# Block sums of the tokens: made over one long chunk or inside the first unit that needs them

## The chip, the cores and the metric

The program runs on one NeuronCore of a Trainium2 chip. TensorE (PE) multiplies, VectorE (DVE) and ScalarE (ACT) do element work between SBUF and the PSUM banks, SyncE (SP) issues plain DMA transfers in the order of its queue, and GpSimd (POOL) issues the accumulating ones and some plain ones. The metric is device time in microseconds for one launch, the median of several runs. A profiled execution of the same program gives the trace that is read below; its times count from the start of the span.

## The reference, cut to what matters

A linear attention over 4 x 576 tokens in 8 heads gives x, 2304 tokens by 512. Two wide layers follow, and these fill most of the time:

```python
x = attention(q, k, v, w_phi)                    # (2304, 512)
gate = 1.0 / (1.0 + np.exp(-(x @ w_gate)))       # w_gate: 512 x 1536
y = (gate * (x @ w_val)) @ w_out                 # layer 1
h = y @ w_in                                     # w_in: 512 x 2048
out = np.maximum(0.01 * h, h) @ w_out2           # layer 2
```

All of it is in fp32 (the weights arrive as 64-bit words and are taken apart on the chip).

## The kernel before, in words

Every fp32 product is made of three PE passes over a high and a low part (L52, L53, L54: high by high, low by high, high by low). ACT makes a high part with a cast, DVE the low part with a subtraction (L48 and L49 for what a unit hands on, called gh and gl).

The tokens stand in five blocks: 0 to 3 with 512 tokens each, and block B (index 4) with 256. The hidden width of a layer is worked through in chunks of 256: six for layer 1 (0 to 5), eight for layer 2 (0 to 7). Chunk 0 of layer 1 runs beside the attention, block by block. Chunk 1 is *plain*: `up_plain` for each of the five blocks, and one step of the weight stream and of the side work behind every group. From chunk 2 on, two blocks make a pair (pair 0 is blocks 0 and 1, pair 1 is blocks 2 and 3), and `quad` computes the two products of a pair in a Strassen-like form: seven products of halves for eight, with sums of the weights (`sh`, `sl`) and sums of the tokens T1 to T4. A *unit* is a pair or block B within a chunk; a pair's unit in layer 1 is two quads, first the gate's, then the value's. The units of chunk 2 are pair 1, B, pair 0, and so back and forth.

The sums of a pair are four DVE subtractions of 128x1024 (`sum_steps`, L739), and for each of the four sums one ACT cast (L749) and one DVE subtraction (L750) into two slots of 128x1024. `ts` holds the sums of one pair. The other pair's lie in HBM (`td`): L756 stores them from the SP queue, and `load_sums` (L791) reads them back from the POOL queue into the same slots, each as soon as its last use is over (`swap`). There are 41 slots of 128x1024 in all, handed out by `take` and returned by `give`; weights, sums and staging share them.

Layer 1's results are gathered in HBM: ACT copies a piece from its PSUM bank into a staging half (L678), and POOL adds it to `accd` (L679). In the last chunk the gathered values are loaded (`acc<-accd`, L663), DVE adds the last piece from PSUM (L682), and ACT and DVE split the result into the xh and xl that layer 2 reads (L685, L686).

Order is set by the text of the program, which each engine follows in its own queue. Down products (`down1_piece`) wait in `pend` and are put between the up products by `gap`; `rooms` says how many at each of a quad's six places. `ahead(n)` takes n steps of `side` (a generator, such as the making of sums) and of the weight stream (`decoded`), and the stream goes on only while more than `reserve` slots are free beside those it takes. A raw weight (`raw`, 512 KB) is loaded by SP at L122, taken apart by DVE at L102 to L114, and its sums are made at L176 to L181. Up products land in the `ps_u` banks (five), down products in the `ps_p` banks (three).

In a quad the order of names is s1 (a copy of a bank by ACT), u2, u3, then the four results; the additions are DVE's (L831), and the value's quad multiplies into the tanh of the gate's (L878).

Of the kernel before, what the change touches and what calls it, by code (L numbers as in the profile page):

```python
# [9 lines left out]
F32 = mybir.dt.float32  # L10
# [9 lines left out]
def linear_attention_moe(ctx, tc, q, k, v, w_phi, w_gate, w_val, w_out, w_in2, w_out2, out):  # L20
# [56 lines left out]
    def give(*slots):  # L77
        free.extend(place for _, place in slots)
# [501 lines left out]
    pools["q"] = ctx.enter_context(tc.tile_pool(name="q", bufs=6))  # L580
# [13 lines left out]
    fixed, halves = [], []  # L594

    def fix(n):
        for _ in range(n):
            s = take(F32)
            fixed.append(s)
            halves.extend(s[0][:, 512 * i:512 * i + 512] for i in range(2))  # L600

    fix(3)
    staged = [0]

    def staging():
        staged[0] += 1
        return halves[staged[0] % 6]
# [123 lines left out]
    td = {}  # L731
# [26 lines left out]
    def first_sums(pair, stay):  # L758

        for i in range(2):  # L760
            for j in range(2):
                s = sums[0, 2 * pair + i, j] = take(F32, "acc")
                nc.sync.dma_start(out=s[0].rearrange("p (k t) -> p k t", k=2), in_=xd[2 * pair + i][:, 2 * j:2 * j + 2])
        for _ in range(14):
            yield True
        yield from sum_steps(1, pair)
        held = deque()

        def put():
            n, s = held.popleft()  # L770
            store_sums(1, pair, n, s)
            if not stay:
                give(*s)

        for n in (2, 1, 3, 4):
            s = [take(F32R) for _ in range(2)]
            sum_parts(1, pair, n, s)
            if stay:
                ts[n] = s
            held.append((n, s))  # L780
            yield True
            yield True
            if len(held) == 2:
                put()
        for _ in range(4):
            yield True
        put()
# [9 lines left out]
    def swap(l, pair, n):  # L797

        ts[n] = [retake(s) for s in ts[n]]
        if (l, pair, n) in td:  # L800
            load_sums(l, pair, n)
        else:
            sum_parts(l, pair, n, ts[n])
            store_sums(l, pair, n, ts[n])
# [66 lines left out]
    def up_pair1(c, pair, between, then):  # L871
        h, th = {}, {}
        for i, t in quad(1, c, 0, pair, (1, 1, 1, 1, 1, 0), lambda n: None):
            th[i] = halves[6 + i]
            nc.scalar.activation(out=th[i], in_=t, func=ACTF.Tanh, scale=0.5)
        between()
        for i, t in quad(1, c, 1, pair, (1, 1, 1, 0, 0, 0), then):
            nc.vector.scalar_tensor_tensor(out=th[i], in0=th[i], scalar=1.0, in1=t, op0=ALU.add, op1=ALU.mult)  # L878
            hidden(h, (i // 2, 2 * pair + i % 2), th[i])
        return h  # L880
# [45 lines left out]
    side.append(first_sums(0, False))  # L926
    for b in range(NB):
        reserve[0] = (4, 8, 8, 5, 2)[b]
        if b == 2:
            for g in side:  # L930
                for _ in g:
                    pass
            side[:] = [first_sums(1, True)]
        h = up_plain(1, 1, b, 5)
        gap(100)
        if b in (1, 3):
            drop_x((b, 0))
        pend.extend(down1_piece(1, b, e, h) for e in range(KD))
    for g in side:
        for _ in g:  # L940
            pass
    side.clear()
    fix(2)
# [3 lines left out]
    pend.append(lambda: drop(1, 1, 2))  # L947

    units = [1, B, 0]
    keep = lambda n: None  # L950
    for c in range(2, NC1):
# [3 lines left out]
        for n, u in enumerate(units):  # L955
            if u == B:
                h = up_plain(1, c, B, 2)
            elif not final:
                h = up_pair1(c, u, (lambda: drop(1, c, 0)) if n == 2 else (lambda: None),
                             (lambda k, u=u: swap(1, 1 - u, k)) if n == 0 else keep)  # L960
            elif u == 0:
                hold[0] = 2, 0
                h = up_pair1(c, 0, lambda: None, lambda k: swap(1, 1, k))
            else:
                def between():
                    gap(100)
                    drop_sums(1, c, 0)
                    give(*fixed[:3])
                    side.append(sum_steps(2, 0))

                def then(k):
                    for g in side:
                        for _ in g:
                            pass
                    side.clear()
                    swap(2, 0, k)
                load_acc(0)
                load_acc(1)
                hold[0] = 2, 1
                h = up_pair1(c, 1, between, then)  # L980
                drop_sums(1, c, 1)
                for b in (2, 3, B):
                    load_acc(b)
                reserve[0] = 0
# [10 lines left out]
    give(*fixed[3:])  # L995

    need(2, 0, 0)
    for _ in sum_steps(2, 1):
        pass
    units = [0, B, 1]  # L1000
    for c in range(NC2):
        for n, u in enumerate(units):
            if u == B:
                h = up_plain(2, c, B, 1)
                gap(3)
            else:
                h = up_pair2(c, u, (lambda k, u=u: swap(2, 1 - u, k)) if n == 0 else keep)
                gap(100)
# [40 lines left out]
```

## Time and profile before

| | us |
|---|---|
| median of 3 runs | 1058.68 (1053.5 to 1058.72) |
| profiled execution | 1057.37 |
| its span | 1055.6 |
| outside the span | 1.77 |
| PE busy in the span | 1024.2 (97%) |
| DVE busy | 779.7 (74%) |
| ACT busy | 519.4 (49%) |
| POOL busy | 170.2 (16%) |

The time is close to PE's busy time, so what can be won without taking work from PE is what PE loses in waits and at a lower clock. Chunk 1 runs from 309.8 us to about 392 us, chunks 2 to 5 follow to about 680 us, and layer 2 fills the rest.

### The profile page before, as it was taken

The page shows a single profiled execution, that of the slowest core. Times are in us where ns is not written, and L with a number is a line of the kernel's source. Part 1 is how long each engine was busy: PE and PEld are TensorE (multiplying, and loading weights), DVE is VectorE, ACT ScalarE, POOL GpSimd, SP SyncE. Part 2 cuts the span into 40 slices and gives each one's busy share as a digit, 9 for nine tenths or more (in the row PEclk, how much of TensorE's full clock was granted, in tenths as well). Part 3 has the DMA queues.
Part 4 walks back from the last instruction along what each step waited for, and adds up shares of the span by engine and source line. Part 5 has one row for each costly group of instructions (what it writes and reads, how often), then busy time and mean ns, then how long its engine had stood idle before and what let it go on. Part 6 is the DMA issues. An engine that isn't in the chain of part 4 may idle for free.

```text
span 1055.6 us, 15004 instructions
## 1 busy us (share of the span) xinstructions
PE 1024.2 (97%) x5410; PEld 870.9 (82%) x5410; DVE 779.7 (74%) x1373; ACT 519.4 (49%) x1066; POOL 170.2 (16%) x217
## 2 busy tenths in 40 slices
PE   8999999999999989999999999899999999999998
PEld 7788989889788778888888878688888888888886
DVE  4964878766489748396684959998797887979555
ACT  4766676767456535454454434477343333433221
POOL 0112121212201123324144120001010010101000
PEclk9999999999999999999999999999999999999999
DMA  6543344332287978759499494536161542515143
GB/s 146 157 98 90 88 101 108 82 104 75 74 296 226 343 141 246 114 145 262 73 239 195 82 317 182 182 139 228 52 237 71 171 149 91 178 62 179 42 165 133
DMA packets 119481, 160.06 MB, mean 152 GB/s; under 512 B 68720, under 2 KB 71408, under 8 KB 119408
## 3 DMA queue, kind: packets, MB, share of 16 engines
q1 hardware_dynamic: 95216, 94.09, 28.5%
q0 software_dynamic: 24192, 65.02, 24.6%
q8 instruction: 43, 0.70, 0.3%
q14 instruction: 30, 0.25, 0.1%
HBM read 109.64 MB, written 49.36 MB: 151 GB/s over the span
## 4 chain that ended last, share of the span: by engine, by line
PE 81%; DVE 8%; DMA 5%; ACT 3%; issue 2%; SPq 1%; POOL 1%; POOLq 0%; DVEq 0%; ACTq 0%
PE ps_u L53 11%; PE ps_u L52 11%; PE ps_u L54 11%; PE ps_p L52 11%; PE ps_p L54 11%; PE ps_p L53 11%; PE kv L395 4%; PE ps_n L445 2%; DMA raw<-in_moe_w_gate_dram 1%; DMA acc<-xd 1%; PE ps_t L328 1%; DVE w L750 1%; DVE ql L430 1%; DVE acc L739 1%; DMA w<-td 1%
## 5 line engine op out<-in xcount | busy, mean ns | idle before, releaser
L831 DVE TENSOR_TENSOR q<-ps_u,q 128x512 f32<-128x512 f32 x160 | 109.6, 686 | 65.6 <-PE ps_u L54 59.4
L53 PE MATMUL ps_u<-xl,w 128*128 128x512 f32 (+1 forms) x432 | 151.6, 351 | 0.3 <-DVE xl L686 0.3
L52 PE MATMUL ps_u<-xh,w 128*128 128x512 f32 (+1 forms) x432 | 151.4, 351 | 0.1
L54 PE MATMUL ps_u<-xh,w 128*128 128x512 f32 (+1 forms) x432 | 150.9, 350 | 0.0
L901 DVE TENSOR_TENSOR acc<-acc,ps_p 128x512 f32<-128x512 f32 x126 | 86.1, 684 | 39.6 <-PE ps_p L54 39.0
L52 PE MATMUL ps_p<-w,gh 128*128 128x512 f32 x288 | 112.2, 390 | 0.0
L53 PE MATMUL ps_p<-w,gh 128*128 128x512 f32 x288 | 112.0, 389 | 0.0
L54 PE MATMUL ps_p<-w,gl 128*128 128x512 f32 x288 | 111.7, 389 | 0.0
L791 POOL DMA_DIRECT2D w<-td x88 | 48.7, 560 | 380.6 <-PE ps_u L54 365.2
L679 POOL DMA_DIRECT2D accd<-w x80 | 70.8, 892 | 229.2 <-ACT w L678 148.3
L52 PE MATMUL ps_u<-w 128*128 128x512 f32 x256 | 100.2, 391 | 1.6 <-DVE q L831 1.6
L53 PE MATMUL ps_u<-w 128*128 128x512 f32 x256 | 99.9, 390 | 0.7 <-DMA w<-td 0.7
L54 PE MATMUL ps_u<-w 128*128 128x512 f32 x256 | 99.7, 389 | 0.0
L52 PEld LDWEIGHTS ps_u<-xh,w 128*128 128x128 f32 x432 | 81.9, 190 | 11.9 <-DVE q L831 0.5
L53 PEld LDWEIGHTS ps_u<-xl,w 128*128 128x128 f32 x432 | 82.0, 190 | 11.4 <-DVE xl L686 0.5
L54 PEld LDWEIGHTS ps_u<-xh,w 128*128 128x128 f32 x432 | 81.9, 190 | 10.9
L52 PE MATMUL ps_p<-gh,w 128*128 128x512 f32 (+1 forms) x216 | 79.3, 373 | 10.3 <-ACT gh L48 4.8
L467 POOL TENSOR_TENSOR rb<-u,rb 64x576 f32<-64x576 f32 x32 | 49.2, 1537 | 233.8 <-DMA rb<-rd 136.3
L717 ACT ACTIVATE q<-q 128x512 f32<-128x512 f32 x48 | 30.2, 632 | 111.9 <-DVE q L831 111.6
L53 PE MATMUL ps_p<-gl,w 128*128 128x512 f32 (+1 forms) x216 | 80.1, 372 | 0.4 <-DVE gl L49 0.4
L54 PE MATMUL ps_p<-gh,w 128*128 128x512 f32 (+1 forms) x216 | 79.7, 370 | 0.0
L49 DVE TENSOR_TENSOR gl<-q,gh 128x512 fp32r<-128x512 f32 (+1 forms) x102 | 61.8, 613 | 20.6 <-ACT gh L48 20.2
(151 smaller groups left out, 2306.0 us busy)
## 6 DMA issues: line engine op xcount, KB each, us to landing
w<-td POOLq DMA_DIRECT2D x88, 512.0 KB, 6.5
td<-w SPq DMA_DIRECT2D x32, 512.0 KB, 5.2
accd<-w POOLq DMA_DIRECT2D x64, 256.0 KB, 6.1
raw<-in_moe_w_out_dram SPq DMA_DIRECT2D x28, 512.0 KB, 4.8
raw<-in_moe_w_in_dram SPq DMA_DIRECT2D x16, 512.0 KB, 4.1
raw<-in_moe_w_gate_dram SPq DMA_DIRECT2D x12, 512.0 KB, 5.9
raw<-in_moe_w_val_dram SPq DMA_DIRECT2D x12, 512.0 KB, 5.1
rb<-rd SPq DMA_DIRECT2D x32, 144.0 KB, 3.2
```

The costliest lines, as they stand in the source:

```text
L49: nc.vector.tensor_tensor(out=lo, in0=src, in1=hi.bitcast(F32), op=ALU.subtract)
L52: nc.tensor.matmul(ps, lh, rh, start=first, stop=False, **kw)
L53: nc.tensor.matmul(ps, lh, rl, start=False, stop=False, **kw)
L54: nc.tensor.matmul(ps, ll, rh, start=False, stop=last, **kw)
L395: nc.tensor.matmul(ps[:, h], p.kf[j // 2][:, j % 2, h, s, :], vf[:, j, 64 * h:64 * h + 65], start=(h, j) == (0, 0), stop=False)
L445: nc.tensor.matmul(ps2, w[0], x[0], start=s == 0, stop=s == 1)
L467: nc.gpsimd.tensor_tensor(out=p.rb[sl], in0=p.u[h][sl], in1=p.rb[sl], op=ALU.mult)
L679: nc.gpsimd.dma_start(out=accd[b][:, e], in_=st, accum_op=ALU.add)
L717: nc.scalar.activation(out=th, in_=t, func=ACTF.Lrelu)
L791: nc.gpsimd.dma_start(out=ts[n][k][0].bitcast(F32), in_=td[l, pair, n][:, k])
L831: nc.vector.tensor_tensor(out=o, in0=x, in1=y, op=ALU.add)
L901: nc.vector.tensor_tensor(out=a, in0=a, in1=po, op=ALU.add)
```

## The change

It moves the making of the token sums, and the room that this needs.

- In chunk 1 only one pair's sums are made, pair 1's, from start to end of the chunk, and they stay in `ts`. Before, pair 0's were made in blocks 0 and 1, stored and given up, and pair 1's from block 2 on.
- Pair 0's tokens are loaded when chunk 1's weights have been dropped (`load_x(0)`), and its sums are made by `make_sums(1, 0, used)` as a side step within the first unit of chunk 2, in the slots of pair 1's, each after its last use. They need no reload there: the eight `w<-td` loads of that swap are gone (88 before, 80 after).
- At the border of the layers, pair 0's sums of layer 2 are side steps of the last value quad, and pair 1's are side steps of layer 2's first unit; before, pair 0's came in one piece at each last use, and the four L739 of pair 1 ahead of layer 2's first quad.
- tanh is written in place (for three of four results) and no longer into fixed staging halves; the `q` ring has seven buffers for six, and there are two fixed slots for three and later five, with four staging halves for six.
- One down piece goes to an earlier place in a quad (rooms), and `reserve` in chunk 1 is lower, so weights may be taken apart further ahead.

```diff
--- before.py
+++ after.py
@@ -577,7 +577,7 @@
     free.extend((wpb, f"v{i}") for i in range(NSLOT - 24))
     pools["dec"] = ctx.enter_context(tc.tile_pool(name="dec", bufs=1))
     pools["hp"] = ctx.enter_context(tc.tile_pool(name="hp", bufs=6))
-    pools["q"] = ctx.enter_context(tc.tile_pool(name="q", bufs=6))
+    pools["q"] = ctx.enter_context(tc.tile_pool(name="q", bufs=7))
     ps_b = ctx.enter_context(tc.tile_pool(name="ps_b", bufs=1, space=PS))
     banks = {"u": [(ps_m, "pg"), (ps_m, "pv")] + [(ps_b, f"u{i}") for i in range(3)], "p": [(ps_m, "po"), (ps_b, "p1"), (ps_b, "p2")]}
     turn = {"u": 0, "p": 0}
@@ -591,20 +591,13 @@
         return pools["q"].tile([128, 512], F32, tag="q", name="q")[:, :w]
 
 
-    fixed, halves = [], []
-
-    def fix(n):
-        for _ in range(n):
-            s = take(F32)
-            fixed.append(s)
-            halves.extend(s[0][:, 512 * i:512 * i + 512] for i in range(2))
-
-    fix(3)
+    fixed = [take(F32) for _ in range(2)]
+    halves = [s[0][:, 512 * i:512 * i + 512] for s in fixed for i in range(2)]
     staged = [0]
 
     def staging():
         staged[0] += 1
-        return halves[staged[0] % 6]
+        return halves[staged[0] % 4]
 
     xs = {}
     for key in xh:
@@ -755,36 +748,42 @@
         for k in range(2):
             nc.sync.dma_start(out=td[l, pair, n][:, k], in_=s[k][0].bitcast(F32))
 
-    def first_sums(pair, stay):
+    def load_x(pair):
 
         for i in range(2):
             for j in range(2):
-                s = sums[0, 2 * pair + i, j] = take(F32, "acc")
-                nc.sync.dma_start(out=s[0].rearrange("p (k t) -> p k t", k=2), in_=xd[2 * pair + i][:, 2 * j:2 * j + 2])
+                t = sums[0, 2 * pair + i, j] = take(F32, "acc")
+                nc.sync.dma_start(out=t[0].rearrange("p (k t) -> p k t", k=2), in_=xd[2 * pair + i][:, 2 * j:2 * j + 2])
+
+    def make_sums(l, pair, used):
+
+        yield from sum_steps(l, pair)
+        late = None
+        for n in (2, 1, 3, 4):
+            while used is not None and n not in used:
+                yield True
+            ts[n] = [take(F32R) for _ in range(2)] if used is None else [retake(t) for t in ts[n]]
+            sum_parts(l, pair, n, ts[n])
+            yield True
+            yield True
+            if late:
+                store_sums(*late)
+            late = l, pair, n, ts[n]
+        for _ in range(2):
+            yield True
+        store_sums(*late)
+
+    def first_sums(pair):
+        load_x(pair)
         for _ in range(14):
             yield True
-        yield from sum_steps(1, pair)
-        held = deque()
-
-        def put():
-            n, s = held.popleft()
-            store_sums(1, pair, n, s)
-            if not stay:
-                give(*s)
-
-        for n in (2, 1, 3, 4):
-            s = [take(F32R) for _ in range(2)]
-            sum_parts(1, pair, n, s)
-            if stay:
-                ts[n] = s
-            held.append((n, s))
-            yield True
-            yield True
-            if len(held) == 2:
-                put()
-        for _ in range(4):
-            yield True
-        put()
+        yield from make_sums(1, pair, None)
+
+    def finish():
+        for g in side:
+            for _ in g:
+                pass
+        side.clear()
 
     def load_sums(l, pair, n):
         for k in range(2):
@@ -797,11 +796,7 @@
     def swap(l, pair, n):
 
         ts[n] = [retake(s) for s in ts[n]]
-        if (l, pair, n) in td:
-            load_sums(l, pair, n)
-        else:
-            sum_parts(l, pair, n, ts[n])
-            store_sums(l, pair, n, ts[n])
+        load_sums(l, pair, n)
 
     def quad(l, c, i, pair, rooms, then):
 
@@ -870,11 +865,11 @@
 
     def up_pair1(c, pair, between, then):
         h, th = {}, {}
-        for i, t in quad(1, c, 0, pair, (1, 1, 1, 1, 1, 0), lambda n: None):
-            th[i] = halves[6 + i]
+        for i, t in quad(1, c, 0, pair, (2, 1, 1, 1, 1, 0), lambda n: None):
+            th[i] = tile2() if i == 0 else t
             nc.scalar.activation(out=th[i], in_=t, func=ACTF.Tanh, scale=0.5)
         between()
-        for i, t in quad(1, c, 1, pair, (1, 1, 1, 0, 0, 0), then):
+        for i, t in quad(1, c, 1, pair, (1, 1, 0, 0, 0, 0), then):
             nc.vector.scalar_tensor_tensor(out=th[i], in0=th[i], scalar=1.0, in1=t, op0=ALU.add, op1=ALU.mult)
             hidden(h, (i // 2, 2 * pair + i % 2), th[i])
         return h
@@ -923,28 +918,20 @@
     for i in range(2):
         drop(1, 0, i)
     pend.append(lambda: drop(1, 0, 2))
-    side.append(first_sums(0, False))
+    side.append(first_sums(1))
     for b in range(NB):
-        reserve[0] = (4, 8, 8, 5, 2)[b]
-        if b == 2:
-            for g in side:
-                for _ in g:
-                    pass
-            side[:] = [first_sums(1, True)]
+        reserve[0] = (4, 4, 0, 0, 0)[b]
         h = up_plain(1, 1, b, 5)
         gap(100)
         if b in (1, 3):
             drop_x((b, 0))
         pend.extend(down1_piece(1, b, e, h) for e in range(KD))
-    for g in side:
-        for _ in g:
-            pass
-    side.clear()
-    fix(2)
+    finish()
     reserve[0] = 0
     for i in range(2):
         drop(1, 1, i)
     pend.append(lambda: drop(1, 1, 2))
+    load_x(0)
 
     units = [1, B, 0]
     keep = lambda n: None
@@ -956,28 +943,31 @@
             if u == B:
                 h = up_plain(1, c, B, 2)
             elif not final:
-                h = up_pair1(c, u, (lambda: drop(1, c, 0)) if n == 2 else (lambda: None),
-                             (lambda k, u=u: swap(1, 1 - u, k)) if n == 0 else keep)
+                done = (lambda: drop(1, c, 0)) if n == 2 else (lambda: None)
+                if c == 2 and n == 0:
+                    used = set()
+                    side.append(make_sums(1, 0, used))
+                    h = up_pair1(c, u, done, used.add)
+                    finish()
+                else:
+                    h = up_pair1(c, u, done, (lambda k, u=u: swap(1, 1 - u, k)) if n == 0 else keep)
             elif u == 0:
                 hold[0] = 2, 0
                 h = up_pair1(c, 0, lambda: None, lambda k: swap(1, 1, k))
             else:
+                used = set()
+
                 def between():
                     gap(100)
                     drop_sums(1, c, 0)
-                    give(*fixed[:3])
-                    side.append(sum_steps(2, 0))
-
-                def then(k):
-                    for g in side:
-                        for _ in g:
-                            pass
-                    side.clear()
-                    swap(2, 0, k)
+                    give(*fixed)
+                    side.append(make_sums(2, 0, used))
+
                 load_acc(0)
                 load_acc(1)
                 hold[0] = 2, 1
-                h = up_pair1(c, 1, between, then)
+                h = up_pair1(c, 1, between, used.add)
+                finish()
                 drop_sums(1, c, 1)
                 for b in (2, 3, B):
                     load_acc(b)
@@ -992,18 +982,21 @@
                 pend.append(lambda c=c: drop(1, c, 2))
         units = units[::-1]
     pend.append(lambda: give(sums.pop((1, B, 0))))
-    give(*fixed[3:])
 
     need(2, 0, 0)
-    for _ in sum_steps(2, 1):
-        pass
     units = [0, B, 1]
     for c in range(NC2):
         for n, u in enumerate(units):
             if u == B:
                 h = up_plain(2, c, B, 1)
                 gap(3)
+            elif c == n == 0:
+                used = set()
+                side.append(make_sums(2, 1, used))
+                h = up_pair2(c, u, used.add)
+                gap(100)
             else:
+                finish()
                 h = up_pair2(c, u, (lambda k, u=u: swap(2, 1 - u, k)) if n == 0 else keep)
                 gap(100)
             if c == n == 0:
```

The lines move by it: what was L739, L749, L750, L756, L763 is now L732, L742, L743, L749, L756; L831 is L826, L878 is L873, L706 is L699, L682 and L686 are L675 and L679, L663 is L656.

The first place is the SP queue from the second half of chunk 1 into chunk 2 (xd_96 and xd_97 are blocks 0 and 1, xd_98 and xd_99 blocks 2 and 3). Before:

```order
L763 DMA acc<-xd_98 128x1024 x2
L763 DMA acc<-xd_99 128x1024 x2
L122 DMA raw<-in_moe_w_out_dram 128x1024
L122 DMA raw<-in_moe_w_gate_dram 128x2x512
L756 DMA td_4445<-w 128x1024 x2
L756 DMA td_4405<-w 128x1024
L756 DMA td_4452<-w 128x1024
L756 DMA td_4405<-w 128x1024
L756 DMA td_4452<-w 128x1024
L756 DMA td_4522<-w 128x1024 x2
L122 DMA raw<-in_moe_w_gate_dram 128x2x512
L122 DMA raw<-in_moe_w_val_dram 128x2x512 x2
```

After:

```order
L122 DMA raw<-in_moe_w_out_dram 128x1024
L122 DMA raw<-in_moe_w_gate_dram 128x2x512 x2
L122 DMA raw<-in_moe_w_val_dram 128x2x512
L756 DMA acc<-xd_96 128x1024
L122 DMA raw<-in_moe_w_val_dram 128x2x512
L122 DMA raw<-in_moe_w_out_dram 128x1024
L756 DMA acc<-xd_96 128x1024
L756 DMA acc<-xd_97 128x1024 x2
L749 DMA td_4737<-w 128x1024 x2
L749 DMA td_4764<-w 128x1024 x2
L749 DMA td_4803<-w 128x1024 x2
```

The four loads of tokens and eight stores that stood between two groups of raw weights in chunk 1 are gone from there; the loads stand after the raw weights, three of the four at the very end of chunk 1, and their stores in a row behind them.

The second place is DVE's queue at the start of chunk 2's first unit (pair 1). The first L831 or L826 is u2 of the gate's quad, the next one u3. Before:

```order
L107 SCALAR_TENSOR_TENSOR m<-raw,m 128x512 x2
L831 TENSOR_TENSOR q<-ps_u,q 128x512
L111 SCALAR_TENSOR_TENSOR m<-m,e 128x512 x2
L102 TENSOR_SCALAR e<-raw 128x512
L114 TENSOR_TENSOR w<-m,w 128x512 x2
L109 SCALAR_TENSOR_TENSOR e<-raw,e 128x512
L831 TENSOR_TENSOR q<-ps_u,q 128x512
L176 TENSOR_TENSOR m<-m 128x2x128
L831 TENSOR_TENSOR q<-ps_u,q 128x512
```

After:

```order
L699 SCALAR_TENSOR_TENSOR q<-q,ps_u 128x256
L49 TENSOR_TENSOR gl<-q,gh 128x256
L826 TENSOR_TENSOR q<-ps_u,q 128x512
L732 TENSOR_TENSOR acc<-acc 128x1024 x4
L826 TENSOR_TENSOR q<-ps_u,q 128x512
L114 TENSOR_TENSOR w<-m,w 128x512
L826 TENSOR_TENSOR q<-ps_u,q 128x512
L114 TENSOR_TENSOR w<-m,w 128x512
L826 TENSOR_TENSOR q<-ps_u,q 128x512
```

The four subtractions over the newly loaded tokens stand now between u2 and u3; the parts of weights (L102 to L114) that stood here have mostly moved ahead.

The third place is DVE's queue at the border of the layers, where the last pieces of layer 1 are added (acc from ps_p) and layer 2's first quad begins. Before:

```order
L114 TENSOR_TENSOR w<-m,w 128x512
L686 TENSOR_TENSOR xl_93<-acc,xh_92 128x512 x2
L739 TENSOR_TENSOR acc<-acc 128x1024
L831 TENSOR_TENSOR q<-ps_u,q 128x512
L739 TENSOR_TENSOR acc<-acc 128x1024
L105 TENSOR_SCALAR m<-raw 128x512
L739 TENSOR_TENSOR acc<-acc 128x1024
L107 SCALAR_TENSOR_TENSOR m<-raw,m 128x512
L739 TENSOR_TENSOR acc<-acc 128x1024
L750 TENSOR_TENSOR w<-acc,w 128x1024
L682 TENSOR_TENSOR acc<-acc,ps_p 128x256 x2
L750 TENSOR_TENSOR w<-acc,w 128x1024
```

After:

```order
L114 TENSOR_TENSOR w<-m,w 128x512
L679 TENSOR_TENSOR xl_93<-acc,xh_92 128x512 x2
L826 TENSOR_TENSOR q<-ps_u,q 128x512
L732 TENSOR_TENSOR acc<-acc 128x1024
L105 TENSOR_SCALAR m<-raw 128x512
L732 TENSOR_TENSOR acc<-acc 128x1024
L107 SCALAR_TENSOR_TENSOR m<-raw,m 128x512
L732 TENSOR_TENSOR acc<-acc 128x1024
L675 TENSOR_TENSOR acc<-acc,ps_p 128x256
L732 TENSOR_TENSOR acc<-acc 128x1024
L679 TENSOR_TENSOR xl_95<-acc,xh_94 128x256
L675 TENSOR_TENSOR acc<-acc,ps_p 128x256
```

The first L675 of 128x256 (block B's sum, which frees a ps_p bank) has three of the four subtractions ahead of it, where L682 had four and one L750. On the SP queue the raw w_out that stood behind the first two `acc<-accd` loads at the end of layer 1 stands ahead of them.

## Rows read from the trace of the kernel before

**Rows 1.** The page, its first part, busy time by engine

```profile
PE 1024.2 (97%) x5410; PEld 870.9 (82%) x5410; DVE 779.7 (74%) x1373; ACT 519.4 (49%) x1066; POOL 170.2 (16%) x217
```

**Rows 2.** Waits of PE: what it waited for, us in total, times, longest

```profile
PE ps_p L52 <- ACT gh L48: 4.8, 3, 3.0
PE ps_p L52 <- DVE acc L682: 4.1, 1, 4.1
...
PE ps_u L52 <- DVE q L831: 1.6, 2, 1.2
```

**Rows 3.** Stretches: us, busy us (x instructions) by engine, clock, DMA share, GB/s

```profile
330.00:360.00 30.00, 30.00 (x134) 24.86 (x133) 24.05 (x34) 15.19 (x23) 7.17 (x8) 1.00 0.98 290
361.50:369.50 8.00, 6.16 (x25) 4.23 (x24) 7.25 (x13) 4.84 (x9) 0.54 (x1) 1.00 1.05 377
378.50:387.00 8.50, 5.25 (x15) 3.69 (x14) 3.17 (x6) 2.86 (x6) 0.87 (x1) 0.80 0.32 62
383.10:386.50 3.40, 3.40 (x8) 2.75 (x9) 0.64 (x2) 0.99 (x2) 0.87 (x1) 0.50 0.00 0
392.00:410.00 18.00, 18.00 (x93) 15.35 (x92) 17.09 (x35) 8.94 (x18) 5.61 (x8) 1.00 0.66 132
676.00:689.00 13.00, 8.23 (x41) 6.69 (x40) 12.98 (x21) 6.20 (x9) 0.00 (x0) 0.87 0.64 233
```

**Rows 4.** Timeline of PE: start, us, instruction, count [idle before <- releaser]

```profile
330.21 0.39 PE L53 MATMUL ps_p<-gl,w 128*128 128x512 f32 x1
330.44 0.39 PE L54 MATMUL ps_p<-gh,w 128*128 128x512 f32 x1
...
382.31 0.51 PE L52 MATMUL ps_p<-gh,w 128*128 128x512 f32 x1 [3.03 <-ACT gh L48]
...
391.31 0.28 PE L54 MATMUL ps_u<-xh,w 128*128 128x256 f32 x1
391.43 0.28 PE L52 MATMUL ps_u<-xh,w 128*128 128x256 f32 x1
```

**Rows 5.** Timeline of DVE in chunk 1

```profile
353.05 1.22 DVE L739 TENSOR_TENSOR acc<-acc 128x1024 f32<-128x1024 f32 x1 [4.77 <-DMA acc<-xd]
...
360.17 1.22 DVE L750 TENSOR_TENSOR w<-acc,w 128x1024 fp32r<-128x1024 f32 x1
361.30 0.68 DVE L706 SCALAR_TENSOR_TENSOR q<-q,ps_u 128x512 f32<-128x512 f32 x1
...
379.10 0.43 DVE L102 TENSOR_SCALAR e<-raw 128x512 int32<-128x512 int32 x1 [3.24 <-DMA raw<-in_moe_w_gate_dram]
...
380.92 0.68 DVE L706 SCALAR_TENSOR_TENSOR q<-q,ps_u 128x512 f32<-128x512 f32 x1
```

**Rows 6.** Timeline of the SP queue: DMA issues, merged, in chunk 1

```profile
340.20 5.48 SPq L763 DMA_DIRECT2D acc<-xd  x4
...
355.39 10.05 SPq L756 DMA_DIRECT2D td<-w  x8
372.26 0.38 SPq L122 DMA_DIRECT2D raw<-in_moe_w_gate_dram  x1
```

**Rows 7.** L763, the four token loads issued at 296.7 to 301.7 us

```profile
DMA to landing us min/median/max: 6.9/7.3/7.8
```

**Rows 8.** Tile xd, the four token loads issued at 340.2 to 344.4 us

```profile
DMA to landing us min/median/max: 8.7/9.6/10.0
```

**Rows 9.** Timeline of DVE, then of PE, at the end of layer 1

```profile
611.65 0.43 DVE L102 TENSOR_SCALAR e<-raw 128x512 int32<-128x512 int32 x1 [6.01 <-DMA raw<-in_moe_w_out_dram]
...
613.91 0.69 DVE L831 TENSOR_TENSOR q<-ps_u,q 128x512 f32<-128x512 f32 x1
...
614.65 0.50 PE L52 MATMUL ps_u<-w 128*128 128x512 f32 x1 [1.20 <-DVE q L831]
```

**Rows 10.** Timeline of DVE, then of PE, at the border of the layers

```profile
676.16 1.21 DVE L739 TENSOR_TENSOR acc<-acc 128x1024 f32<-128x1024 f32 x1
...
682.24 1.22 DVE L750 TENSOR_TENSOR w<-acc,w 128x1024 fp32r<-128x1024 f32 x1
683.38 0.74 DVE L682 TENSOR_TENSOR acc<-acc,ps_p 128x256 f32<-128x256 f32 x2
...
683.84 0.58 PE L52 MATMUL ps_p<-gh,w 128*128 128x256 f32 x1 [4.14 <-DVE acc L682]
```

**Rows 11.** L679, the accumulating DMAs of 410 to 600 us

```profile
DMA to landing us min/median/max: 2.9/5.8/8.5
```

**Rows 12.** Timeline of ACT: copies into the staging halves in chunk 2

```profile
419.49 1.10 ACT L678 COPY w<-ps_p 128x512 f32<-128x512 f32 x2
...
426.98 0.59 ACT L678 COPY w<-ps_p 128x512 f32<-128x512 f32 x1 [0.46 <-PE ps_p L54]
```

## The prediction

> **What bounds the kernel now.** I read the page's first part first: PE is busy for 1024.2 of 1055.6 us [rows 1], and the change takes no matmul away. So its worth is in what PE loses, about 31 us in all, and I ask which of that lies where the change works. The list of PE's waits gives three lines for layers 1 and 2: a down product waiting for an ACT cast, longest 3.0 us; one waiting for a DVE addition, 4.1 us once; an up product waiting for a DVE addition, 1.6 us [rows 2].
>
> Then the stretches around these. A 128x512 matmul starts every 0.227 us and a 128x256 one every 0.12 us where PE runs freely [rows 4]. Between 361.5 and 369.5 us PE started 25 matmuls of 128x512, 5.7 us of work, so 2.3 us are lost; between 378.5 and 387.0 us it started 15, 3.4 us of work, so 5.1 us are lost [rows 3]. Part of the second loss is clock: from 383.1 to 386.5 us the granted clock is 0.50, that is 1.2 GHz for 2.4, and 3.4 us at that rate cost 1.7 [rows 3]. It comes just after PE stood still for 3.03 us [rows 4]. **Chunk 1 loses 7.4 us** in these two places.
>
> What is late there? DVE waited 4.77 us for the token loads at 353.05, then did eight sums of 128x1024 in a row, and the L706 that PE's next hidden block needs stood behind them until 361.30 [rows 5]. The loads had been issued from 340.2 on and took 8.7 to 10.0 us; the eight stores of the sums held SP from 355.4 for 10 us, so that the next raw weight was issued only at 372.26 [rows 6, 8]. DVE waited for it until 379.10, with L706 behind at 380.92 [rows 5], and PE's 3.03-us wait ends a little after that. The stretch is one with much DMA: 98% of the engines' time in 330 to 360 us [rows 3]. So the second round of sums in chunk 1 is late by its loads, and its stores make the weights late.
>
> Two smaller places: at 614.65 PE waited 1.20 us for a DVE addition that had stood behind a wait of 6.01 us for a raw w_out [rows 9]; and at the border of the layers 4.14 us for the L682 at 683.38, which had four L739 and an L750 ahead of it [rows 10].
>
> **The change part by part.**
>
> *Chunk 1, gain 7.4 us.* One of its two rounds leaves: four L739 and four L750 at 1.13 us from one start to the next (9 us of DVE), four ACT casts, four loads and eight stores of 512 KB. The remaining round is loaded before the chunk, as the first one was, and with less traffic. The raw weights move up on SP past all of the stores; DVE then has neither the 4.77-us nor the 3.24-us wait, and no run of eight ahead of L706. At 24.05 of 30 us in 330 to 360 [rows 3], it keeps room when 9 us leave. I count all 7.4; the other end is 2.3, if the weights stay late (the second place) and only the run of sums goes.
>
> *Chunk 2's first unit, cost 1.4 us for the loads.* The loads of pair 0's tokens can go only into slots that chunk 1's weights give up, so three of four are issued with its last up products, about 0.5 us before the unit begins. Nothing in the trace shows a load at this place. The nearest rows are the same four loads in two other places: 6.9 to 7.8 us (median 7.3) and, in the crowd, 8.7 to 10.0 [rows 7, 8]. The four subtractions stand between u2 and u3 on DVE, so behind the last landing come about three more steps of 1.13 and the 0.7 of u3, 4.1 us. PE reaches the group that takes u3's bank after 30 matmuls of 128x512 and 24 of 128x256, 6.8 + 2.9 = 9.7 us from the unit's start. With 7.3 the sum is 6.8 + 4.1 = 10.9, 1.2 late, and I add 0.2 for the hand-over: 1.4. With 6.9 it is 1.0, with 10.0 it is 4.1, and then a stretch at half clock may follow as it did after 3.03 us, 1.7 more: 5.8. I take 7.3, since before this place the crowd of stores is gone. Behind the waiting DVE row stand u3 and two parts of a weight, all needed later than u3 itself.
>
> The Trainium skill, "SBUF — State Buffer", section "The DMA setup-cost knee", gives 2 us plus bytes at 436 GB/s for a transfer; for the three loads together that would be an estimate of 5.6 us, no wait at all, and the whole sum 1.4 us lower. The trace speaks against it where other traffic runs: 6.9 at the least for such a load [rows 7].
>
> *The rest of that unit, cost 1.0 us.* 9 us of DVE work come into a stretch where DVE was busy 17.09 of 18.0 us without making PE wait [rows 3]. What keeps it from overflowing is that the parts of weights that filled it are ahead now, as the order shows (L102 to L111 gone from between the additions). Were none of them moved, 17.1 + 9.1 − 18.0 = 8.2 us would fall on PE; were all moved, nothing. Following rows against the groups that wait for them, each comes about in time; I put 1.0.
>
> *The end of layer 1, gain 1.2 us.* The raw w_out is issued ahead of the `acc<-accd` load that it stood behind, so the 6-us wait of DVE and PE's 1.20 behind it go [rows 9]. Bounds 0 and 1.2.
>
> *Border of the layers, gain 1.5 us.* DVE is busy 12.98 of 13.0 us in 676 to 689 [rows 3], so it sets the pace there. Ahead of the L682 that PE waits for, one L739 and one L750 fewer (2.3 us), and some parts of weights done earlier (I find some 2.5 us of rows). So most of the 4.14 us goes. But what left the front of that addition stands now between it and the next two additions of block B, which PE needs within 3 us: two L743 and an L114, 2.9 us. The wait is cut into pieces, and the third addition comes some 1.5 us earlier than before. Bounds: 0, if the backlog is only handed on; 5.8, if it goes whole (4.14 and the 1.7 of a half-clock stretch behind it).
>
> *At nothing:* tanh in place changes no instruction, only tiles; seven `q` buffers cover the longer life of one. Eight POOL loads of 512 KB leave chunk 2 and eight SP stores come in; both lie beside PE's work. One piece of `rooms` moves by one place. *Staging of four halves:* a copy now waits for the DMA of the fourth before it. In chunk 2 that copy comes 7.5 us later (419.49 to 426.98, [rows 12]), and 0.6 us of it is the copy itself, ahead of its DMA; the median DMA of 5.8 us [rows 11] has landed by then, the longest, 8.5, has not, by 1.6. Three ps_p banks give about two groups of 1.36 us before PE feels it. So nothing, with the other end below.
>
> *Sum.* 7.4 + 1.2 + 1.5 = 10.1 gained, 1.4 + 1.0 = 2.4 lost: 7.7 less. The profiled execution, 1057.4, becomes 1049.7; the median lies 1.3 above it, so **1051.0 us**, 0.7% faster. Its own range, from the bounds: 1045 (the border whole, the unit free) to 1056 (loads 4.1 late).
>
> **The rivals.**
>
> *The gain is given back at chunk 2's first unit* (0.17). DVE's load there speaks for it (17.09 of 18.0), the order against it. With 8.2 us instead of 1.0: 1051 + 7.2 = 1058; with half of that 1054.6; with 8.2 and the loads 4.1 late 1061.
>
> *The change doesn't free chunk 1* (0.13). The stalls would belong to the DMA engines' 98%, not to the sums: raw weights come late anyway, 5.1 us stay: 1056. For it: the DMA engines are that full already in 330 to 360, before PE loses anything. Against it: it is the second round's loads and the last stores of the first that fill this stretch.
>
> *Slower, by the staging halves* (0.08). If the accumulating DMAs of chunks 1 to 4 land like their longest, 8.5 us, each group of four copies is 1.6 us late; there are 20 such groups (five blocks with four pieces each in four chunks), and at 0.9 us on PE each they cost 18: 1069. At 0.4 us each the 7.7 us are used up, from 0.65 on the kernel is slower. Against it: the median of 5.8 and three banks.
>
> *The border goes whole* (0.10): 4.3 more than in the sum, 1046.7.
>
> **How the numbers follow.** The forecast has 0.52. Half a per cent, 5.3 us, is about what a measurement of this kernel tells from no change, so faster means below 1053.4. Of the forecast nine tenths lie there (0.47), the whole border adds 0.10, and of the first two rivals about a fifth (0.06): 0.63. Slower, above 1064, takes the staging and a small part of the first rival where everything is late with a half clock: 0.09. The rest, 0.28, is no change. The range of 1043 to 1060 leaves out the staging, a tail of the first rival, and a gain of more than 15.
>
> **What would show it.** Right: in chunk 1 no wait of PE above 1 us and no half clock near its end; a DVE wait for `acc<-xd` at the start of chunk 2, with a PE wait of 1 to 2 us for the u3 addition L826 some 10 us into the unit; no wait near the raw w_out of the last chunk; at the border, waits for L675, L678 and L679 of under 2.5 us each. Wrong: PE waiting for `raw` or L699 in chunk 1; a wait over 3 us for u3 and a clock of 0.50 behind it; ACT waiting for POOL's accumulating DMAs in L671, with PE waiting for ps_p in chunks 2 to 5.

## The result: 1.1% slower

The changed kernel takes 1070.37 us in the median of 4 runs (1069.35 to 1074.19), beside 1058.7 for before on the same chip (1053.5 to 1062.04). The ratio is 1.0113, interval 1.0086 to 1.0141. Forecast were 1051 us and a range of 1043 to 1060.

PE's busy time first, then its waits, longest in total first (answers to [rows 1, 2]):

```profile
PE 1030.9 (96%) x5410; PEld 876.7 (82%) x5410; DVE 779.9 (73%) x1373; ACT 519.6 (48%) x1066; POOL 164.9 (15%) x209
```

```profile
PE ps_u L52 <- DVE q L826: 12.4, 3, 4.5
...
PE ps_u L52 <- ACT xh L678: 2.4, 1, 2.4
PE ps_p L52 <- ACT gh L48: 1.8, 1, 1.8
PE ps_u L52 <- DMA w<-td: 1.7, 1, 1.7
```

The wait for L48 in chunk 1 (3.0 us) and that for the addition at the border (4.1 us) are gone; the 1.8 left for L48 ends at 304 us, ahead of chunk 1. In their place stand three waits of PE for a DVE addition L826, 12.4 us together. Where they lie is told by the stretches: chunk 1, chunk 2's first unit, the first units of chunks 3 and 4, the end of layer 1, and the border (same columns as [rows 3]):

```profile
310.00:388.00 78.00, 77.96 (x388) 66.22 (x388) 60.31 (x107) 42.02 (x72) 14.40 (x16) 1.00 0.82 207
388.00:412.00 24.00, 20.26 (x94) 16.68 (x93) 14.80 (x20) 9.71 (x16) 3.52 (x4) 0.93 0.53 138
478.00:495.00 17.00, 12.88 (x58) 10.60 (x57) 11.01 (x21) 4.31 (x9) 3.58 (x6) 0.80 0.92 312
553.00:575.00 22.00, 17.47 (x84) 14.59 (x84) 11.98 (x23) 7.42 (x14) 6.46 (x10) 0.84 0.86 262
640.00:660.00 20.00, 17.10 (x68) 13.38 (x67) 11.31 (x17) 4.77 (x8) 0.00 (x0) 0.91 0.51 184
690.00:712.00 22.00, 18.31 (x81) 14.73 (x80) 20.44 (x32) 12.74 (x21) 0.00 (x0) 0.84 0.56 216
```

Chunk 1 runs through without a loss, as forecast: 77.96 of 78 us. But every other stretch loses PE time and clock. Counted as starts of matmuls against PE's free pace [rows 4], 388 to 412 loses 5.7 us, 478 to 495 6.5 and 553 to 575 6.8, and in none of these three did before lose anything. Before, around chunks 3 and 4:

```profile
470.00:500.00 30.00, 30.00 (x157) 25.78 (x156) 20.46 (x38) 13.55 (x25) 11.63 (x17) 1.00 1.02 268
545.00:575.00 30.00, 30.00 (x162) 26.01 (x161) 16.21 (x29) 12.93 (x24) 12.22 (x17) 1.00 1.04 248
```

With 2.3 us more at the end of layer 1, 1.1 more at the border, about 1.8 in a stretch of half clock at 304 to 312 us (two of the eight variants below show it as well, so it is not put down to the change), and 8.1 less in and around chunk 1, the sum is 16 of the 17 us by which the two profiled executions differ. That of the changed kernel is the slowest of its four, 1074.19 us; the medians differ by 12.

The two stretches at chunks 3 and 4 are alike, and nothing in the prediction speaks of them. DVE at the first of them, then PE:

```profile
473.64 0.69 DVE L107 SCALAR_TENSOR_TENSOR m<-raw,m 128x512 f32<-128x512 uint32 x1
...
476.04 0.42 DVE L102 TENSOR_SCALAR e<-raw 128x512 int32<-128x512 int32 x1
...
482.13 0.43 DVE L102 TENSOR_SCALAR e<-raw 128x512 int32<-128x512 int32 x1 [4.13 <-DMA raw<-in_moe_w_out_dram]
482.47 1.29 DVE L114 TENSOR_TENSOR w<-m,w 128x512 fp32r<-128x512 f32 x2
483.68 0.69 DVE L109 SCALAR_TENSOR_TENSOR e<-raw,e 128x512 int32<-128x512 int32 x1
484.28 0.69 DVE L826 TENSOR_TENSOR q<-ps_u,q 128x512 f32<-128x512 f32 x1
```

```profile
485.02 0.80 PE L52 MATMUL ps_u<-w 128*128 128x512 f32 x1 [4.12 <-DVE q L826]
```

DVE stands for 4.13 us at L102, the first step of taking a weight apart, and the addition that PE needs is the fourth instruction behind it. The weight is the second half of a w_out. The SP queue shows when it was asked for (two issues merged, the second at the end of the stretch), the waits of that queue in 468 to 478 us what held it back, and the answer for the tile raw how long the load took:

```profile
463.23 11.46 SPq L122 DMA_DIRECT2D raw<-in_moe_w_out_dram  x2
```

```profile
SPq L122 <- DVE m L107: 10.7, 1, 10.7
```

```profile
DMA to landing us min/median/max: 7.7/7.7/7.7
```

It was issued 0.3 us before 474.7, as soon as the L107 at 473.64 had read the raw buffer that it goes into: SP had waited 10.7 us for that. DVE came to the L102 that reads it at 478.0 (482.13 less the wait): 3.6 us for a load that takes 7.7 in the stretch where POOL reads the other pair's sums back. My expectation below says 2 us, which is too short. At 557.8 us the same happens once more, with 4.54 us.

Chunk 2's first unit shows the wait that was forecast, larger (DVE, then the three loads issued at 385.6 to 387.9, then PE):

```profile
389.98 0.69 DVE L826 TENSOR_TENSOR q<-ps_u,q 128x512 f32<-128x512 f32 x1 [1.43 <-PE ps_u L54]
394.91 5.06 DVE L732 TENSOR_TENSOR acc<-acc 128x1024 f32<-128x1024 f32 x4 [4.24 <-DMA acc<-xd]
399.89 0.68 DVE L826 TENSOR_TENSOR q<-ps_u,q 128x512 f32<-128x512 f32 x1
```

```profile
DMA to landing us min/median/max: 6.4/8.7/8.9
```

```profile
400.63 0.50 PE L52 MATMUL ps_u<-w 128*128 128x512 f32 x1 [3.74 <-DVE q L826]
```

### The profile page after: what moved, and what is told of

Its sections match the earlier page's. It is cut to its first block, busy times and chain, and to the rows that moved or that the text cites. A ratio compares the mean times of both kernels' runs of the same rounds, so it can differ in the third digit from the quotient of the medians.

```text
span 1072.4 us, 14962 instructions
## 1 busy us (share of the span) xinstructions
PE 1030.9 (96%) x5410; PEld 876.7 (82%) x5410; DVE 779.9 (73%) x1373; ACT 519.6 (48%) x1066; POOL 164.9 (15%) x209
## 4 chain that ended last, share of the span: by engine, by line
PE 80%; DVE 7%; DMA 6%; ACT 4%; SPq 2%; issue 1%; POOL 1%; POOLq 0%; DVEq 0%; ACTq 0%
PE ps_u L52 12%; PE ps_u L53 12%; PE ps_u L54 12%; PE ps_p L52 11%; PE ps_p L54 11%; PE ps_p L53 11%; PE kv L395 4%; PE ps_n L445 2%; DMA raw<-in_moe_w_out_dram 2%; DMA raw<-in_moe_w_gate_dram 1%; DVE ql L430 1%; DMA w<-td 1%; POOL rb L467 1%; DMA acc<-xd 1%; ACT qh L416 1%
## 5 line engine op out<-in xcount | busy, mean ns | idle before, releaser
L826 DVE TENSOR_TENSOR q<-ps_u,q 128x512 f32<-128x512 f32 x160 | 110.0, 688 | 63.1 <-PE ps_u L54 54.2
L52 PE MATMUL ps_u<-w 128*128 128x512 f32 x256 | 102.1, 399 | 14.1 <-DVE q L826 12.4
L53 PE MATMUL ps_u<-w 128*128 128x512 f32 x256 | 101.5, 397 | 1.2 <-DMA w<-td 1.2
L790 POOL DMA_DIRECT2D w<-td x80 | 44.0, 558 | 378.3 <-PE ps_u L54 267.2
L54 PE MATMUL ps_u<-w 128*128 128x512 f32 x256 | 101.7, 397 | 0.0
L48 ACT CAST gh<-q 128x512 fp32r<-128x512 f32 (+1 forms) x134 | 75.1, 575 | 52.8 <-DVE q L873 35.9
L49 DVE TENSOR_TENSOR gl<-q,gh 128x512 fp32r<-128x512 f32 (+1 forms) x134 | 82.9, 632 | 21.3 <-ACT gh L48 21.1
L54 PE MATMUL ps_p<-gh,w 128*128 128x512 f32 (+1 forms) x216 | 80.1, 371 | 0.0
```

What stands on the lines that cost most here:

```text
L48: nc.scalar.copy(hi, src)
L49: nc.vector.tensor_tensor(out=lo, in0=src, in1=hi.bitcast(F32), op=ALU.subtract)
L52: nc.tensor.matmul(ps, lh, rh, start=first, stop=False, **kw)
L53: nc.tensor.matmul(ps, lh, rl, start=False, stop=False, **kw)
L54: nc.tensor.matmul(ps, ll, rh, start=False, stop=last, **kw)
L790: nc.gpsimd.dma_start(out=ts[n][k][0].bitcast(F32), in_=td[l, pair, n][:, k])
```

## The experiments

Theory A: the new waits at chunks 3 and 4 come from the weight stream, which has run ahead until a raw load that is issued too late stands in front of PE's addition. Rival B: they come from the crowd of transfers or from the sums themselves. Theory C: the wait at 396 us is the late landing of the token loads; rival D: DVE is too full there. Each ratio is to runs of before on the same chip.

**The rooms back.** This undoes two lines of the change and nothing else:

```diff
-quad(1, c, 0, pair, (2, 1, 1, 1, 1, 0), ...)
+quad(1, c, 0, pair, (1, 1, 1, 1, 1, 0), ...)
-quad(1, c, 1, pair, (1, 1, 0, 0, 0, 0), then)
+quad(1, c, 1, pair, (1, 1, 1, 0, 0, 0), then)
```

> The changed kernel with the places of the down pieces in a quad as before (one, one, one, one, one, none and one, one, one, none). In the order of its build the second L102 of the w_out of the chunk after next moves from ahead of the value quad's u2 addition to behind the whole first unit, in chunks 3 and 4 alike. Theory A (the waits of 4.1 and 4.5 us at 480 and 556 us are DVE standing at L102 for a raw w_out that was issued 2 us earlier beside the w<-td loads, with the addition for PE queued behind): both waits and the half-clock stretches behind them go, 6.5 + 6.8 = 13.3 us less, about 1057. Rival B (the crowd of DMA traffic in the first unit, or the sums, make the additions late whatever stands in front): the waits stay, 1070. The wait of 3.7 us at 396 us stays under both.

Measured: 1054.78 us, ratio 0.9944 (0.9924 to 0.9964), against 1.0113 for the whole change: 1.7% or 18 us less. DVE in chunk 3's first unit, and two stretches:

```profile
479.12 0.69 DVE L826 TENSOR_TENSOR q<-ps_u,q 128x512 f32<-128x512 f32 x1
...
480.92 0.69 DVE L826 TENSOR_TENSOR q<-ps_u,q 128x512 f32<-128x512 f32 x1
...
485.71 0.42 DVE L102 TENSOR_SCALAR e<-raw 128x512 int32<-128x512 int32 x1
```

```profile
470.00:500.00 30.00, 30.00 (x158) 25.86 (x158) 17.54 (x34) 13.90 (x25) 12.46 (x18) 1.00 1.00 255
545.00:575.00 30.00, 30.00 (x167) 26.22 (x166) 13.67 (x26) 13.21 (x25) 11.81 (x15) 1.00 1.01 225
```

The L102 comes behind the additions now and waits for nothing; PE loses nothing in either stretch, with the DMA engines 100% busy. So B falls. The wait at 396 us did not stay as expected: it is 2.46 us here, with the clock at 1.00. Why places of down pieces move a weight is in the code: `down1_piece` calls `ahead(1)` behind its products, one step of the weight stream. A piece that comes earlier takes its step earlier, and here that decided on which side of the additions the L102 stands.

**The slots back.**

```diff
     fixed = [take(F32) for _ in range(2)]
+    spare = [take(F32)]
...
-        reserve[0] = (4, 4, 0, 0, 0)[b]
+        reserve[0] = (4, 8, 8, 5, 2)[b]
...
     finish()
+    spare.extend(take(F32) for _ in range(2))
...
```

> The changed kernel with three slots of 128x1024 taken and never used (one from the start, two after chunk 1, given back where before gave its staging back) and the reserve of chunk 1 as before (4, 8, 8, 5, 2), so the weight stream has as many free slots as in before; the rooms stay as changed. The L102 of that w_out stands again behind the first unit. Theory A, with the freed slots as the reason that the stream runs ahead: the waits at 480 and 556 go, 13 us less, about 1057. Rival (the rooms alone move it, or the waits have another cause): 1070. Chunk 1 stays without a long wait under both if its gain came from the sums; if it came from weights taken apart further ahead, some of 7 us come back there.

Measured: 1063.0 us, ratio 1.0018 (0.9992 to 1.0045), 10 us less than the whole change.

```profile
470.00:500.00 30.00, 30.00 (x156) 25.79 (x156) 21.90 (x42) 14.19 (x25) 11.65 (x16) 1.00 1.01 281
```

The waits at chunks 3 and 4 are gone here too, and chunk 1 keeps its gain, so that gain is not the weights' being further ahead. The wait at 396 us stays (3.08 us), and others of about 3 us stand at 618 us (2.73) and at the border (3.01), so less is gained than with the rooms back. So freed slots (with chunk 1's reserve, which this run also takes back) and moved pieces do it together: either one taken back is enough.

**The token loads one block earlier.**

```diff
-        reserve[0] = (4, 4, 0, 0, 0)[b]
+        reserve[0] = (4, 4, 4, 4, 0)[b]
+        if b == 4:
+            load_x(0)
...
-    load_x(0)
```

> The changed kernel with pair 0's four token loads issued ahead of block B's part of chunk 1 and not after it; the reserve of chunk 1 becomes (4, 4, 4, 4, 0), so that four slots are free there. In its order the four subtractions no longer stand between u2 and u3 of chunk 2's first unit. Theory C (the 3.74 us of PE at 396 us, and the half clock behind, are the late landing of these loads): they go, 5.7 us less, about 1064.5, with the waits at 480 and 556 as they are. Rival D (DVE is too full in that unit, whatever the loads): a wait of 2 us or more comes back later in the unit and less than 3 us are gained.

Measured: ratio 1.0048 (1.0026 to 1.0071), 0.65% or 7 us less than the whole change.

```profile
384.00:408.00 24.00, 23.79 (x126) 19.92 (x125) 22.53 (x40) 13.53 (x23) 4.42 (x5) 1.00 0.81 205
```

PE loses next to nothing in chunk 2's first unit, with DVE 94% busy. C holds and D falls. A wait of 1.35 us appears behind it, at 431 us.

**Both together.**

> Both of the edits together: rooms as before and the token loads one block earlier. If theories A and C hold and the two do not touch each other, 13.3 + 5.7 = 19 us less than the changed kernel: about 1051, faster than before by some 0.7%. If B or D holds, 1064 or more.

Measured: 1052.25 us, ratio 0.9918 (0.9889 to 0.9947). This is 2% less than the whole change, where the single edits give 1.7 and 0.65; with intervals this wide it is not shown whether the two gains add up in full.

**Four raw buffers.** A and its rival A2 (the place in the order alone) are told apart by an earlier load with both L102 left in front of the addition:

```diff
-        raws = deque(fetch(keys[n // 2], n % 2, 3) for n in range(3))
+        raws = deque(fetch(keys[n // 2], n % 2, 4) for n in range(4))
-                ahead = 2 * n + i + 3
+                ahead = 2 * n + i + 4
...
-    NSLOT = 41
+    NSLOT = 40
```

> The changed kernel, its rooms too, with four raw buffers for three (and 40 slots for 41): each raw weight is loaded one step ahead of where it was. In its order the L102 of the w_out stands at the same place of chunk 3's and 4's first unit, in front of the addition. Theory A (the late issue of the load is what matters): the waits at 480 and 556 us go although the order is the same there, 13 us less, about 1057. Rival A2 (it is the place in the order, and in the crowd the load would be late whenever it is issued) or B (traffic): they stay, 1069 to 1071. The wait of 3.7 us at 396 stays, and chunk 1 stays without a wait.

Measured: 1056.99 us, ratio 0.9975 (0.995 to 1.0), 14 us less. SP, and DVE in chunk 3's first unit:

```profile
463.30 3.42 SPq L122 DMA_DIRECT2D raw<-in_moe_w_out_dram  x2
```

```profile
479.32 0.42 DVE L102 TENSOR_SCALAR e<-raw 128x512 int32<-128x512 int32 x1
...
480.37 0.50 DVE L102 TENSOR_SCALAR e<-raw 128x512 int32<-128x512 int32 x1
...
482.46 0.69 DVE L826 TENSOR_TENSOR q<-ps_u,q 128x512 f32<-128x512 f32 x1
```

Both L102 still stand ahead of the addition (two L114 that stood behind the second L102 now follow the addition, and there is one slot less), but the second load is issued at 466 us and not at 474, and no one waits, though the load took 8.0 us. A2 falls: the place does harm only while the load is issued that late, and it is so late because the third raw buffer is not free before. The wait at 396 us did not stay as it was here but grew to 5.26 us, with the token loads at 8.8 to 12.7 us, as theory C would have it; the 14 us are what is left after that:

```profile
388.00:412.00 24.00, 18.74 (x83) 15.36 (x82) 12.58 (x17) 8.00 (x14) 3.49 (x4) 0.86 0.50 133
```

**The rooms alone, on the kernel before.** The two `rooms` lines of the change and nothing else.

> The kernel before with nothing changed but the places of the down pieces in a quad (two first, then one each; and one, one, none). With before's slots the order of L102 is the same as in before there. If the rooms do harm only together with the freed slots: no change, 1056 to 1064 beside the before of the same chip. If they do harm by themselves: 8 us or more slower.

Measured: ratio 1.0013 (0.9991 to 1.0036). No harm by themselves, and no loss of PE around chunks 3 and 4. The profiled execution, the slowest of ten, has longer waits than before at two of before's own places (4.33 us for 3.03 in chunk 1, 4.92 for 1.20 at the raw w_out of the last chunk); the ten times together show no difference.

**Layer 2's sums as before,** on the fast variant. It puts `sum_steps(2, 1)` ahead of the first quad again and makes pair 0's sums at each last use.

> The fast variant (rooms as before, token loads one block earlier) with the sums of layer 2 made as in before: pair 0's in one piece at each last use, pair 1's four L732 ahead of layer 2's first quad. If the change's handling of these sums is worth the 1.5 us forecast (pieces of waits in place of one): 1 to 2 us slower than the fast variant, with one wait of 3 to 4 us at the border as in before. If worth nothing: within 1 us of the fast variant. If it costs: faster.

Measured: ratio 0.9906 (0.9873 to 0.9938) beside 0.9918, the same within the intervals. The wait of 3 to 4 us that I expected is not there either; the longest at the border is 1.0 us:

```profile
660.00:690.00 30.00, 27.73 (x143) 22.91 (x143) 29.54 (x48) 16.10 (x27) 0.00 (x0) 1.00 0.47 175
```

So the times show no gain from the change's handling of these sums, and the traces speak against it: by the count of starts the border loses 3.9 us here and 7.9 in the fast variant. That this does not show in the profiled times has a plain reason: the same matmul ahead of chunk 1 starts at 306.20 us here and at 301.63 there, in a part where the two kernels do not differ. What made before's wait of 4.14 us is not settled by this run.

**Layer 2's sums later.**

```diff
             elif c == n == 0:
-                used = set()
-                side.append(make_sums(2, 1, used))
-                h = up_pair2(c, u, used.add)
+                h = up_pair2(c, u, keep)
+                side.append(make_sums(2, 1, {1, 2, 3, 4}))
                 gap(100)
```

> The fast variant with pair 1's sums of layer 2 begun only behind the first quad of layer 2, so that on DVE no L732 and L743 of that pair stand between the last additions of layer 1 and the split that PE waits for. The border now loses some 7 us there, 2.4 of it one wait for an ACT cast and the rest shorter waits and a half clock of 6.8 us. If the backlog of DVE is the cause: most of it goes, 4 to 6 us less than the fast variant, 1047 or so; the sums then come late for pair 1's quad, which may give 1 to 3 back. If the late thing is the gathered values and not DVE: no change at the border.

Measured: 1045.9 us, ratio 0.9871 (0.983 to 0.9912), the fastest of all. The border in the fast variant, then here:

```profile
660.00:690.00 30.00, 26.75 (x122) 21.93 (x121) 28.31 (x47) 17.08 (x29) 0.00 (x0) 0.89 0.41 158
```

```profile
660.00:690.00 30.00, 30.00 (x156) 25.65 (x155) 29.11 (x49) 19.33 (x34) 0.00 (x0) 1.00 0.24 87
```

DVE is as busy, and PE loses nothing, where by the count of starts the fast variant loses 7.9 us: it was what stood in front, not how much there was. The ratio is 0.5% below that of the fast variant, 5 us, but the two intervals overlap, so the trace of the border and not the time is the evidence.

## Why the prediction was wrong

**Chunk 1** held in effect and size: 7.4 us forecast, 8.1 measured. The 7.4 was a little low because the (x25) and (x15) of [rows 3] count matmuls that reach into the stretch; 23 and 13 start in it, which makes 8.3. One step of its account was misread: the stores did not hold up the raw weight of 372.26 us. SP was through with them at 365.4 [rows 6] and then waited for DVE to read the raw buffer; before, 362 to 374 us:

```profile
SPq L122 <- DVE m L107: 6.7, 1, 6.7
```

So the trace of before already held a raw load that was late by its ring of three buffers, with what PE needs behind it on DVE.

**The failed step** is the sentence under "at nothing": "One piece of `rooms` moves by one place." With it fell the premise that chunks 3 and 4, where before loses nothing, would stay as they were. I asked what work an edit removes or moves, and an edit that only changes numbers in a tuple moved the L102 of a w_out in front of an addition, together with the three freed slots. It cost the two stretches of 6.5 and 6.8 us, each a wait of PE for an addition behind a raw load issued too late (4.12 and 4.53 us) with a half clock after it. The pieces taken back gave 18 us, which is more than both: the profiled execution lost 1 to 3 us less at four other places too (304, 396 and 640 us and the border), and why is open. Freed slots I had put down to more room for weights, as a gain, and did not follow where the stream would then stand in chunks 3 and 4. The order of the build shows it, and I read it only at the places that I had picked from the trace of before.

**The token loads** were the right mechanism and mis-sized: 1.4 us forecast with 7.3 us from issue to landing; they took up to 8.9 and PE's wait was 3.74, inside my bound of 4.1, with a stretch of half clock behind: 5.7 in all, against 5.8 at that bound. The Trainium skill's rule for a transfer ("SBUF — State Buffer", "The DMA setup-cost knee"), weighed there, was further off, with an estimate of 5.6 us for three loads together and no wait at all, against 6.4 to 8.9 us for each. I chose the calm rows because the stores were gone; but the place was not calm: the DMA engines were 100% busy from 385 to 397 us. Accumulating DMAs of the last block run beside these loads; that they are what made them late is not shown.

**The rest of that unit** cost next to nothing: with the loads early, PE ran through it (0.8 us lost in 24, where 1.0 was forecast).

**The end of layer 1:** the wait for the raw w_out went, as forecast, but PE waited for `w<-td` instead, 1.72 and 1.19 us with a half clock behind: 2.3 us lost more than before where 1.2 were to be gained. What made these loads late there is not shown.

**The border:** the forecast form came out, waits in pieces of under 2.5 us (0.68, 0.53, 2.37), but not the gain of 1.5, nor even its lower bound of 0: 1.1 us more were lost than before, because the 2.37 was followed by about 6.8 us at half clock, where before had 3.4, and I had tied half clock to waits of over 3 us. The run with the sums of layer 2 as before loses less there, and the one with the sums later loses nothing: what had to move was the subtractions and the L743 of pair 1, which the prediction left among the additions that PE waits for. The same shows at 644 us, where a half clock came after 1.72 and 1.19 us.

**The rivals:** loads late, as in the first rival, did come, but its price was put on DVE's fullness, which the run with early loads excludes. The staging halves did no harm: in the changed kernel and its variants no wait of PE for a `ps_p` bank appears in chunks 2 to 4.

## What to carry to other kernels

Where side work is stepped by the main work, a number that says when to step is an edit to every later place in the order: compare the order over the whole program, and look for waits on DMA that have moved in front of something that PE needs, not only at the places where the old trace shows stalls. A load that is issued when its buffer comes free is only as early as that buffer, so one more buffer (14 us here) and a later place for its reader (18 us) repair the same wait. When a backlog stands at a border, ask which of it may come after the border: with the same sums moved behind the first quad, the 7.9 us that PE lost there were gone from the trace.

## What the runs showed of the hardware

The granted clock fell after shorter waits than the 3.03 and 4.14 us of before's trace, and the length of one wait does not tell whether it falls. In the changed kernel two waits of 1.72 and 1.19 us, with 0.5 us of matmuls between them, were followed by 3.4 us at half clock (0.91 in the mean of 640 to 660 us); with the rooms back, a single wait of 2.46 us left it at 1.00:

```profile
388.00:412.00 24.00, 20.92 (x104) 17.19 (x104) 17.98 (x25) 9.84 (x15) 3.50 (x4) 1.00 0.62 187
```

Nor does it tell how long the half clock lasts. After the waits of 4.1 and 4.5 us the mean clock of the two stretches is 0.80 and 0.84, which is about 6.8 us at half clock each, and after the 3.74 us at 400 us it is 0.93 of 24 us, 3.4. The same wait of 2.37 us at the border, behind two short ones of about 0.5 and 0.7 us, was followed by about 6.8 us in the changed kernel (0.84 of 690 to 712 us) and by about 3.4 with four raw buffers (0.91 of 680 to 700 us).
